# One batch's sums over U and the next batch's first local scores in one group on TensorE, the sums laid out by halves of the channels

## The chip, the cores and the metric

The kernel runs on one core of a Trainium2 chip. The metric is the device time of one execution in microseconds; lower is better. Profiles name the engines: PE (TensorE's matmuls) and PEld (its weight loads), DVE (VectorE), ACT (ScalarE), POOL (GpSimd) and SP, whose queue issues the DMAs.

## What is computed

Sparse attention, a low-rank mix along the sequence, and an MLP, in float32, for 8 batches of 576 positions, 8 heads of 64 channels (512 channels in all):

```python
# attention: heads 0-3 local (the last 32 positions), heads 4-7 strided (positions 32 apart)
scores = q @ k.T / sqrt(64)                      # masked: local or strided
x = softmax(scores) @ v                          # then heads side by side: [8, 576, 512]
# mix along the sequence, rank 32: U [576, 32], V [32, 576]
h = x.transpose(0, 2, 1) @ U @ V
u = x + h.transpose(0, 2, 1)
# MLP over the channels, 512 -> 2048 -> 512
out = u + relu(u @ w_ch1) @ w_ch2
```

## The kernel before

**Blocks.** The 8 x 576 positions are cut into nine blocks of 512: block n has the first 512 positions of batch n, and block 8 the 64 last positions (the tails) of all batches. A block's MLP is 16 steps (fc) of twelve matmuls of the first layer (`ph<-uh,w` and `ph<-ul,w`; u and the weights are split into a high and a low part) and, two steps behind (`LAG`), twelve of the second (`acc<-gh,w`, `acc<-gl,w`), each 128x512. Four evictions `o<-acc,ul` by VectorE end a block's second layer, so they fall into the beginning of the next block.

**Attention beside it.** While block n = 1 to 6 runs, batch b = n + 1 is prepared. A block is 64 ticks (four per fc), and `plan` (at L851) says from which tick a task runs; in a tick `tick` lets each task take a step. TensorE's order is the order of this code (`tensor.on` is true); the other engines and SP are ordered by the scheduler. All small products write the tile px, of which there is one (`ps_x`, two banks of 512 columns; `psx2`).

- "pairs": the four local heads, two at a time. `attention_pair` (L320) loads keys and queries (kT, qT) and values (vt); `masked` (L214) issues 36 score matmuls, each 64 rows by 32 columns of the array, in eight places side by side (two row groups by four column groups) into columns 0 to 319 of both banks; `masked_shifted` (L223) adds the mask, takes the maximum and subtracts it (s_sb); then come the exponential, a transpose (blocks), a store to DRAM (pd), a fetch in another layout (PT), 36 products with the values (`outputs`, px<-vt,PT) and the division into x_loc. Pair 0's scores stand at tick 3, pair 1's at 13, the products at 20 and 34.
- "str" or heads: `strided_heads` (L356), the four strided heads on POOL (products tmp) and VectorE (their sums s_st), from the tick `EARLY` of the block before; results in x_str.
- "mix": `mix_both` (L470), at tick 47 (51 in block 1), forms the sums over U: x (positions x channels) is the moving operand, U the stationary one with 32 columns. The 576 positions are five pieces: four of 128 rows, which go to four column groups, and one of 64, whose four matmuls cover 64 channels each. x_loc and x_str give 256 channels each. The four partial sums (32 partitions each) are added by one copy of ACT and three additions of VectorE (`st<-px`), and split into tst.
- "u0", "u1": `u_local` and `u_strided` multiply by V (`px<-Vst,tst`, two matmuls 96x512 each) and add x (`xT<-px,xT`, `xS<-px,xS`), which gives the next block's u.
- `tail_products` (L604): four Vst matmuls of 64 columns for the 64 last positions of the batch before, in columns 320 to 447 of px, behind the scores of pair 0 (`due`, `tail_out`).

**Buffers.** The pool "att" has seven buffers (`ATT_BUFS`) for kT, qT, s_sb, blocks, PT, xT, xS, tmp, tl and o, each taken as one comes free; vt has one buffer. A product of POOL, an eviction or a load waits until a buffer is free.

Of the kernel before, what the change touches and what calls it, by code (L numbers as in the profile page):

```python
# [7 lines left out]
F32 = mybir.dt.float32  # L8
# [6 lines left out]
ALU = mybir.AluOpType  # L15
AX = mybir.AxisListType
NEG = -1.0e9
B, H, S, D = 8, 8, 576, 64
DM, FF, R = 512, 2048, 32
NCH = S // 32  # L20
# [5 lines left out]
NSP = 2  # L26
LAG = 2
EARLY = 58


ATT_BUFS = 7
# [16 lines left out]
def fused_kernel(ctx, tc, fqk, lqk, lv, eqk, ev, sqkv, U, V, wts, masks, eye, out):  # L48
# [4 lines left out]
    ap_ = ctx.enter_context(tc.tile_pool(name="ap", bufs=1))  # L53
# [24 lines left out]
    def att(shape, name, dtype=F32):  # L78
        return ap_.tile(shape, dtype, name=name, tag="att", bufs=ATT_BUFS)
# [3 lines left out]
    def psx2():  # L83
        banks["n"] += 1
        if banks["prefix"] and banks["n"] % 3:
            return ps_acc.tile([128, 2, 512], F32, name="acc")
        return ps_x.tile([128, 2, 512], F32, name="px")
# [3 lines left out]
    def dma(out, in_):  # L91
        with tc.issue_after(last_dma[0]) if InOrder.on and last_dma[0] is not None else nullcontext():
            last_dma[0] = nc.sync.dma_start(out=out, in_=in_).ins  # L93
# [4 lines left out]
    masks_sb = const.tile([128, 768 + D + 1], BF16, name="masks_sb")  # L98
# [113 lines left out]
    due = []  # L212

    def masked(kT, qT, sp):  # L214
        for c in range(NCH):
            t, c4 = c // 4, c % 4
            for hh, rows in enumerate(halves):
                key = kT[rows, 32 * c - 32:32 * c + 32] if c else kT[rows, None, 0:32].broadcast_to([64, 2, 32])
                tensor.matmul(sp[32 * c4:32 * c4 + 32, hh, 64 * t:64 * t + 64], qT[rows, 32 * c:32 * c + 32], key,
                                 start=True, stop=True, skip_group_check=True, tile_position=(64 * hh, 32 * c4))  # L220
        return sp[:, :, 0:320].rearrange("p h (t x) -> p h t x", x=64)

    def masked_shifted(sp, mask):  # L223
        s_sb = att([128, 5, 2, 64], "s_sb")
        mx = ap_.tile([128, 16], F32, name="mx", bufs=2)[:, 0:10].rearrange("p (h t) -> p h t", h=2)
        s_v = s_sb.rearrange("p t h x -> p h t x")
        m = mask.rearrange("p (t x) -> p t x", x=64)[:, None]
        nc.gpsimd.memset(s_sb[64:128, 4], 0.0)
        for n, ts in ((128, slice(0, 4)), (64, slice(4, 5))):
            vector.tensor_tensor(out=s_v[0:n, :, ts], in0=sp[0:n, :, ts],  # L230
                                 in1=m[0:n, :, ts].broadcast_to([n, 2, ts.stop - ts.start, 64]), op=ALU.add)
        vector.tensor_reduce(out=mx, in_=s_v, axis=AX.X, op=ALU.max)
        vector.tensor_tensor(out=s_v, in0=s_v, in1=mx.broadcast_to([128, 2, 5, 64]), op=ALU.subtract)
        return s_sb

    def shifted(sp):
        s_sb = att([128, 5, 2, 64], "s_sb")
# [6 lines left out]
    def exponentials(s_sb):  # L244
        scalar.activation(out=s_sb, in_=s_sb, func=AF.Exp, scale=0.125)
# [9 lines left out]
    def turned(view, store):  # L255
        blocks = att([128, 640], "blocks")
        vector.transpose(out=blocks.rearrange("p (e t s) -> p t e s", e=4, s=32), in_=view)
        for e in range(4):
            dma(out=store[e].rearrange("k c x -> c k x"), in_=blocks[:, 160 * e:160 * e + 160])

    def fetched(store, name):
        got = att([128, 640], name)
        dma(out=got, in_=store.rearrange("e k c x -> (e k) (c x)"))
        return got
# [36 lines left out]
                vector.tensor_tensor(out=dst, in0=o[:, hh, :, 0:D].rearrange("p t (e x) -> p t e x", e=2),  # L301
                                        in1=rb[:, hh].rearrange("p t (e x) -> p t e x", e=2), op=ALU.mult)

    def pair_loads(b, pr, bufs=None):
        src, values = (lqk[b, pr], lv[b, pr]) if pr < 2 else (eqk[b, pr - 2], ev[b, pr - 2])
        if bufs is None:
            kT, qT = att([128, S], "kT"), att([128, S], "qT")
            full = ap_.tile([128, NCH, D + 1], F32, name="vt", tag="vt")
            dma(out=kT, in_=src[0])
            dma(out=qT, in_=src[1])  # L310
            dma(out=full.rearrange("p c x -> p (c x)"), in_=values)
            return kT, qT, lambda c: full[:, c]
        kT, qT, v0, v1 = bufs
        dma(out=kT, in_=src[0])
        dma(out=qT, in_=src[1])
        for n, part in enumerate((v0, v1)):
            dma(out=part.rearrange("p c x -> p (c x)"), in_=values[:, 9 * (D + 1) * n:9 * (D + 1) * (n + 1)])
        return kT, qT, lambda c: (v0, v1)[c // 9][:, c % 9]

    def attention_pair(b, pr, loaded=None):  # L320
        if loaded is None:
            loaded = pair_loads(b, pr)
            for _ in range(3 + 6 * pr):
                yield
        kT, qT, vt = loaded
        px = psx2()
        sp = masked(kT, qT, px)
        last = due.pop() if due else None
        if last is not None:
            tail_products(last, px)  # L330
        yield
        s_sb = masked_shifted(sp, masks_sb[:, 0:320])
        if last is not None:
            tail_out(last, px)
        yield
        exponentials(s_sb)
        yield
        yield
        turned(s_sb.rearrange("p t h (e x) -> p t (h e) x", x=32), p_store[pr])
        yield  # L340
        yield
        PT = fetched(p_store[pr], "PT")
        for _ in range(11 + 4 * pr):
            yield
        op = outputs(PT, vt, lambda c: 160 * (c % 4) + 32 * (c // 4))
        yield
        normalised(op, pr)
        yield
        turned(x_loc[:, :, 128 * pr:128 * pr + 128].rearrange("p t (e x) -> p t e x", x=32), x_store[pr])
        yield  # L350


# [115 lines left out]
        vector.tensor_tensor(out=dst[64:96], in0=ps, in1=dst[0:32].bitcast(F32), op=ALU.subtract)  # L468

    def mix_both(b):  # L470
        ps = psx2()[:, :, 0:256]
        for half, x in enumerate((x_loc, x_str)):
            for j in range(4):
                tensor.matmul(ps[32 * j:32 * j + 32, half], U_sb[:, 0, j, :], x[:, j, :], start=True, stop=False,
                                 skip_group_check=True, tile_position=(0, 32 * j))
        for half, x in enumerate((x_loc, x_str)):
            for j in range(4):
                part = slice(64 * j, 64 * j + 64)
                tensor.matmul(ps[32 * j:32 * j + 32, half, part], U_sb[0:64, 0, 4, :], x[0:64, 4, part], start=False,
                                 stop=True, skip_group_check=True, tile_position=(0, 32 * j))  # L480
        ta = sums_in[b].rearrange("p (h d) -> p h d", h=2)
        scalar.copy(out=ta, in_=ps[0:32])
        for j in range(1, 4):
            vector.tensor_tensor(out=ta, in0=ps[32 * j:32 * j + 32], in1=ta, op=ALU.add)
        tsts[b] = ap_.tile([96, DM], F32R, name="tst")
        dst = tsts[b].rearrange("p (h d) -> p h d", h=2)
        scalar.copy(out=dst[0:32], in_=ta)
        scalar.copy(out=dst[32:64], in_=ta)
        vector.tensor_tensor(out=dst[64:96], in0=ta, in1=dst[0:32].bitcast(F32), op=ALU.subtract)
# [114 lines left out]
    def tail_products(b, px):  # L604
        for half, ps in enumerate(tail_space(px)):
            for dc in range(2):
                mixed(ps[:, dc], b, 2 * half + dc, Vst, TB, S, True)

    def tail_out(b, px):
        (p0, p1), tl = tail_space(px), tail_of(b)  # L610
        vector.tensor_tensor(out=tl[:, 0:2], in0=p0, in1=tl[:, 0:2], op=ALU.add)
        for e in range(2):
            vector.tensor_tensor(out=tl[:, 2 + e], in0=p1[:, e], in1=o_str[b][e][:, TB:S], op=ALU.add)
        dma(out=rest[:, :, 64 * b:64 * b + 64], in_=tl)
# [209 lines left out]
    def task(gen, key, start, rate=1.0, after=()):  # L824
        return [gen, key, start, rate, after, 0.0]

    def calls(*fns):
        for fn in fns:
            fn()
            yield  # L830

    def plan(n):
        b = n + 1
        if b < B:
            return [
                task(run_staggered([attention_pair(b, 0), attention_pair(b, 1)], 4), "pairs", 0, 1.0),
                task(calls(lambda: mix_both(b)), "mix", 51 if n == 1 else 47, 1.0, ("pairs", "str")),
                task(u_local(b), "u0", 51 if n == 1 else 48, 1.0, ("mix",)),
                task(calls(lambda: u_strided(b), lambda: None, lambda: tail_begin(b)), "u1", 58 if n == 1 else 55, 1.0,
                     ("mix", "u0")),  # L840
            ]
        if b == B:
            return [task(last_tail(), "tail", 2), task(u_rest(), "rest", 12, 1.0, ("tail",))]
        return []
# [216 lines left out]
```

## Time and profile before

| | us |
|---|---|
| median of three runs | 893.72 (893.64 to 895.8) |
| the profiled execution, own time | 894.76 |
| its span on the profile | 892.7 |
| ahead of and behind the span | 2.06 |
| one block (from 333.6 to 428.2 on the profile) | 94.6 |
| scores, all 864 records of `px<-kT,qT` 64x64 | 11.8 busy |
| sums over U, 112 records of 128x256 and 112 of 64x64 | 13.1 busy |

The profile was taken in one execution; the granted clock of TensorE was 0.998. A row of a timeline has the start in us from the span's start, the busy time, the engine, the line (L70 is a helper through which most instructions are issued, so rows are told apart by the tiles), what is written and read, and how many instructions were put together (xN). Float32 matmuls of the attention take two passes, so each is two records. In brackets stands how long the engine idled ahead and what ended it. Busy times of pipelined matmuls overlap; starts are sounder than ends.

### The profile page before, as it was taken

What the parts mean: (1) busy time and instruction counts of PE and PEld (TensorE: products, weight loads), DVE (VectorE), ACT (ScalarE), POOL (GpSimd) and SP (SyncE); (2) the same over time, 40 slices, a digit from 0 to 9 for tenths busy, and PEclk for the clock granted to TensorE, in tenths of its full rate; (3) what the DMA queues carried; (4) which work ended last, traced back from release to release, by engine and by line L of the source; (5) the groups of instructions that cost most, each with busy time, mean ns of one, the idle gap of its engine ahead of it and who ended that gap; (6) DMA issues with size and microseconds to landing.
All of it is one profiled execution on the core that took longest, in us unless ns stands there. A gap on an engine that the chain in (4) does not pass through costs nothing.

```text
span 892.7 us, 16196 instructions
## 1 busy us (share of the span) xinstructions
PE 881.7 (99%) x6625; PEld 708.1 (79%) x6625; DVE 523.9 (59%) x953; ACT 257.8 (29%) x501; POOL 376.9 (42%) x398
## 2 busy tenths in 40 slices
PE   7999999999999999999999999999999999999998
PEld 4677778887878788878888788878887888888886
DVE  5998875766677656766577566756767331112112
ACT  6866751115212521142114311331015221111110
POOL 2000014964796368665668366926854120002000
PEclk9999999999999999999999999999999999999999
DMA  9991111222223223331232313232231030001001
GB/s 353 406 404 63 55 60 54 85 92 71 85 81 121 80 67 97 99 96 59 89 93 77 104 50 121 67 101 60 81 96 48 1 101 0 1 1 48 1 0 48
DMA packets 45914, 80.63 MB, mean 90 GB/s; under 512 B 10736, under 2 KB 23536, under 8 KB 45840
## 3 DMA queue, kind: packets, MB, share of 16 engines
q1 hardware_dynamic: 45840, 79.60, 26.7%
q8 instruction: 52, 0.85, 0.4%
q14 instruction: 22, 0.18, 0.1%
HBM read 61.23 MB, written 18.35 MB: 89 GB/s over the span
## 4 chain that ended last, share of the span: by engine, by line
PE 94%; DVE 2%; DMA 2%; POOL 1%; SPq 1%; issue 0%; DVEq 0%
PE acc L70 44%; PE ph L70 44%; PE px L70 6%; DMA raw_u<-in_U_dram 1%; DMA raw<-in_wts_dram 1%; POOL tmp L374 1%; SPq L93 1%; DVE s_st L70 0%; DVE ul L70 0%; DVE s_sb L70 0%; DVE o L70 0%; DVE xS L70 0%; DVE x_str L70 0%; DVE x_loc L70 0%; DVE mx L70 0%
## 5 line engine op out<-in xcount | busy, mean ns | idle before, releaser
L70 PE MATMUL ph<-uh,w 128*128 128x512 f32 x1152 | 384.8, 392 | 0.0
L70 PE MATMUL acc<-gh,w 128*128 128x512 f32 x1152 | 382.8, 392 | 0.5 <-DVE o L70 0.5
L374 POOL TENSOR_TENSOR tmp<-st,st 128x576 f32<-128x576 f32 (+6 forms) x162 | 175.4, 1112 | 236.9 <-DMA st<-in_sqkv_dram 154.1
L70 PEld LDWEIGHTS acc<-gh,w 128*128 128x128 f32 x1152 | 216.3, 188 | 47.4 <-issue 0.9
L70 PEld LDWEIGHTS ph<-uh,w 128*128 128x128 f32 x1152 | 216.2, 188 | 47.1 <-DVE gl L70 0.5
L70 PE MATMUL ph<-ul,w 128*128 128x512 f32 x576 | 224.3, 389 | 0.0
L70 PE MATMUL acc<-gl,w 128*128 128x512 f32 x576 | 224.3, 389 | 0.0
L70 ACT ACTIVATE gh<-ph 128x512 fp32r<-128x512 f32 x144 | 86.0, 598 | 456.2 <-PE ph L70 450.5
L70 DVE SCALAR_TENSOR_TENSOR gl<-ph,gh 128x512 fp32r<-128x512 f32 x144 | 98.6, 686 | 177.8 <-ACT gh L70 177.4
L400 POOL TENSOR_TENSOR tmp<-st,s_st 128x448 f32<-128x448 f32 (+7 forms) x162 | 137.1, 943 | 52.8 <-DVE s_st L70 30.3
L70 DVE TENSOR_REDUCE s_st<-tmp 128x9 f32<-128x576 f32 (+6 forms) x162 | 90.5, 570 | 59.9 <-POOL tmp L374 56.9
L70 PEld LDWEIGHTS ph<-ul,w 128*128 128x128 f32 x576 | 108.2, 188 | 21.9
L70 PEld LDWEIGHTS acc<-gl,w 128*128 128x128 f32 x576 | 108.1, 188 | 21.8
L70 DVE TENSOR_REDUCE st<-tmp 128x64 f32<-128x64 f32 (+8 forms) x162 | 90.8, 569 | 40.2 <-POOL tmp L400 37.9
L704 POOL TENSOR_TENSOR o<-o,uh 128x512 f32<-128x512 f32 x32 | 40.4, 1297 | 115.1 <-DVE o L70 115.1
L70 ACT COPY x_str<-st 32x256 f32<-32x256 f32 (+1 forms) x144 | 50.5, 351 | 43.1 <-DVE st L70 41.4
L70 ACT ACTIVATE s_sb<-s_sb 128x640 f32<-128x640 f32 x20 | 14.8, 738 | 41.8 <-DVE s_sb L70 39.5
L70 DVE TENSOR_TENSOR st<-px,st 32x512 f32<-32x512 f32 x18 | 12.4, 686 | 21.5 <-ACT st L70 21.1
L70 DVE SCALAR_TENSOR_TENSOR raw<-raw 128x512 int32<-128x512 int32 x32 | 22.0, 688 | 3.7 <-ACT raw L70 3.5
L70 DVE SCALAR_TENSOR_TENSOR cv<-cv,raw 128x512 int32<-128x512 int32 x32 | 22.2, 693 | 1.1
L70 DVE TENSOR_TENSOR w<-cv,w 128x512 fp32r<-128x512 f32 x32 | 21.8, 684 | 0.9 <-ACT w L70 0.9
L70 DVE TENSOR_TENSOR o<-acc,ul 128x512 f32<-128x512 f32 x32 | 20.6, 680 | 2.6 <-DMA out_dram<-o 2.1
(127 smaller groups left out, 484.3 us busy)
## 6 DMA issues: line engine op xcount, KB each, us to landing
raw<-in_wts_dram SPq DMA_DIRECT2D x32, 512.0 KB
st<-in_sqkv_dram SPq DMA_DIRECT2D x18, 576.0 KB
out_dram<-o SPq DMA_DIRECT2D x35, 256.0 KB
vt<-in_lv_dram SPq DMA_DIRECT2D x14, 585.0 KB
pd<-blocks SPq DMA_DIRECT2D x48, 80.0 KB
PT<-pd SPq DMA_DIRECT2D x12, 320.0 KB
xd<-blocks SPq DMA_DIRECT2D x48, 80.0 KB
xT<-xd SPq DMA_DIRECT2D x12, 320.0 KB
```

Source lines behind the costliest of these rows:

```text
L70: r = op(*args, **kwargs)
L93: last_dma[0] = nc.sync.dma_start(out=out, in_=in_).ins
L374: nc.gpsimd.tensor_tensor(out=tmp[:, 0:n], in0=sk[:, j0:j0 + n], in1=sq[:, i:i + 1].broadcast_to([128, n, D]), op=ALU.mult)
L400: nc.gpsimd.tensor_tensor(out=tv.rearrange("p d j -> p j d"), in0=sv[:, 0:i + 1, d0:d0 + step], in1=s_st[:, i, 0:i + 1].broadcast_to([128, ...
L704: nc.gpsimd.tensor_tensor(out=o, in0=o, in1=uh[:, m].bitcast(F32), op=ALU.add)
```

## The change

1. `mix_both(b)` for b = 2 to 6 (blocks 1 to 5) first issues the 36 score matmuls of pair 0 of batch b + 1, into columns 0 to 319 of the same px tile; the sums stand in columns 320 to 447. The keys are loaded by a new task, "keys", at tick 39. `with_mask` (two additions of VectorE) reads the scores right after the sums were added; s_sb is kept until the next block.
2. The sums are laid out by halves of the channels: a column group holds 128 channels of x_loc and of x_str (two banks) for two of the four pieces of positions. Sixteen matmuls of 128 channels replace eight of 256. The last piece has eight matmuls 64 wide as before, now with 128 rows. Two partial sums per half are added: twice a copy of ACT and an addition of VectorE over 256 columns.
3. Timing of the pairs is in a table, `PAIR_TICKS`. For batches whose first scores were early (3 to 7, blocks 2 to 6) pair 0 has no score group of its own; pair 1's scores stand at tick 7 (before 13) and carry the tail's four matmuls; PT is fetched later (own ticks 14 and 28); products stand at 20 and, in the block's ticks, 35.

```diff
+PAIR_TICKS = (((3, 3, 14, 20), (13, 10, 28, 34)), ((2, 2, 14, 20), (6, 5, 28, 34)))
...
+    early_keys, early_scores, early_first = {}, {}, set()
...
+    def attention_pair(b, pr):
+        early, own = b in early_first, {}
...
+        def scores():
+            px = psx2()
+            sp = px[:, :, 0:320].rearrange("p h (t x) -> p h t x", x=64)
+            masked(*own["keys"], sp)
+            last = due.pop() if due else None
+            if last is not None:
+                tail_products(last, px)
+            own["s"] = with_mask(sp, masks_sb[:, 0:320])
...
+        at = PAIR_TICKS[early][pr]
+        if early and pr == 0:
+            steps = [(6, values), (at[0], saved)]
+        else:
+            steps = [(at[0] - at[1], keys), (0 if pr == 0 else 22, values), (at[0], scores)]
+        steps += [(at[0] + 1, lambda: shift(own["s"])), (at[0] + 2, lambda: exponentials(own["s"])), (at[0] + 4, store),
+                  (at[2], fetch), (at[3], products), (at[3] + 1, lambda: normalised(own["o"], pr)), (at[3] + 2, turn_x)]
...
     def mix_both(b):
-        ps = psx2()[:, :, 0:256]
-        for half, x in enumerate((x_loc, x_str)):
-            for j in range(4):
-                tensor.matmul(ps[32 * j:32 * j + 32, half], U_sb[:, 0, j, :], x[:, j, :], start=True, stop=False,
-                                 skip_group_check=True, tile_position=(0, 32 * j))
-        for half, x in enumerate((x_loc, x_str)):
-            for j in range(4):
-                part = slice(64 * j, 64 * j + 64)
-                tensor.matmul(ps[32 * j:32 * j + 32, half, part], U_sb[0:64, 0, 4, :], x[0:64, 4, part], start=False,
-                                 stop=True, skip_group_check=True, tile_position=(0, 32 * j))
-        ta = sums_in[b].rearrange("p (h d) -> p h d", h=2)
-        scalar.copy(out=ta, in_=ps[0:32])
-        for j in range(1, 4):
-            vector.tensor_tensor(out=ta, in0=ps[32 * j:32 * j + 32], in1=ta, op=ALU.add)
+        px = psx2()
+        ps, xs = px[:, :, 320:448], (x_loc, x_str)
+        sp = px[:, :, 0:320].rearrange("p h (t x) -> p h t x", x=64)
+        if b + 1 < B:
+            masked(*early_keys.pop(b + 1), sp)
+        for j in range(4):
+            for half in range(2):
+                for c in range(2):
+                    g = 64 * c + 32 * (j % 2)
+                    tensor.matmul(ps[g:g + 32, half], U_sb[:, 0, j, :], xs[half][:, j, 128 * c:128 * c + 128], start=j < 2,
+                                     stop=False, skip_group_check=True, tile_position=(0, g))
+        for j in range(2):
+            for half in range(2):
+                for c in range(2):
+                    g, x0 = 64 * c + 32 * j, 64 * j
+                    tensor.matmul(ps[g:g + 32, half, x0:x0 + 64], U_sb[:, 0, 4, :],
+                                     xs[half][:, 4, 128 * c + x0:128 * c + x0 + 64], start=False, stop=True,
+                                     skip_group_check=True, tile_position=(0, g))
+        ta = sums_in[b]
+        for c in range(2):
+            half_ta = ta.rearrange("p (h c x) -> p h c x", h=2, c=2)[:, :, c]
+            scalar.copy(out=half_ta, in_=ps[64 * c:64 * c + 32])
+            vector.tensor_tensor(out=half_ta, in0=ps[64 * c + 32:64 * c + 64], in1=half_ta, op=ALU.add)
...
+        if b + 1 < B:
+            early_first.add(b + 1)
+            early_scores[b + 1] = with_mask(sp, masks_sb[:, 0:320])
...
-                task(run_staggered([attention_pair(b, 0), attention_pair(b, 1)], 4), "pairs", 0, 1.0),
-                task(calls(lambda: mix_both(b)), "mix", 51 if n == 1 else 47, 1.0, ("pairs", "str")),
+                task(run_staggered([attention_pair(b, 0), attention_pair(b, 1)], 1), "pairs", 0, 1.0),
+                task(calls(lambda: mix_both(b)), "mix", 51 if n == 1 else 47, 1.0, ("pairs", "str", "keys")),
+                task(calls(lambda: early_keys.update({b + 1: load_keys(b + 1, 0)} if b + 1 < B else {})), "keys", 39, 1.0,
+                     ("pairs",)),
```

The order on PE in the last quarter of block 1 (`w_3`: the MLP's steps 12 to 15; then the part of the weights, and a buffer's number). Before:

```order
L70 MATMUL ph<-uh,w_3_1_1524 128x512
L70 MATMUL ph<-ul,w_3_1_1524 128x512
L70 MATMUL ph<-uh,w_3_1_1524 128x512
L70 MATMUL px<-x_loc,U_sb 32x256 x4
L70 MATMUL px<-x_str,U_sb 32x256 x4
L70 MATMUL px<-x_loc,U_sb 32x64 x4
L70 MATMUL px<-x_str,U_sb 32x64 x4
L70 MATMUL ph<-uh,w_3_2_1405 128x512
```

With the change, whose helper lines are one further down (the sums' rows alternate on between x_loc and x_str, four times 128 wide and twice 64 wide):

```order
L71 MATMUL ph<-ul,w_3_1_1524 128x512
L71 MATMUL ph<-uh,w_3_1_1524 128x512
L71 MATMUL px<-kT,qT 32x64 x36
L71 MATMUL px<-x_loc,U_sb 32x128 x2
L71 MATMUL px<-x_str,U_sb 32x128 x2
...
L71 MATMUL px<-x_loc,U_sb 32x64 x2
L71 MATMUL px<-x_str,U_sb 32x64 x2
L71 MATMUL ph<-uh,w_3_2_1405 128x512
```

The scores stand ahead of the sums in one group between the same two steps of the MLP. On PE at the beginning of block 2, where the second layer of block 1 ends and the first of block 2's begins its round (`w_0_0`), before:

```order
L70 MATMUL acc<-gl,w_3_2_1711 128x512
L70 MATMUL acc<-gh,w_3_2_1711 128x512
L70 MATMUL px<-kT,qT 32x64 x36
L70 MATMUL px<-Vst,tst 128x64 x4
L70 MATMUL ph<-uh,w_0_0_479 128x512
L70 MATMUL ph<-ul,w_0_0_479 128x512
```

With the change:

```order
L71 MATMUL acc<-gl,w_3_3_1731 128x512
L71 MATMUL acc<-gh,w_3_3_1731 128x512
L71 MATMUL px<-kT,qT 32x64 x36
L71 MATMUL px<-Vst,tst 128x64 x4
L71 MATMUL ph<-uh,w_0_0_479 128x512
L71 MATMUL ph<-ul,w_0_0_479 128x512
```

There the first group was pair 0's; it is now pair 1's, one step of the MLP later (`w_3_3` for `w_3_2`), and pair 0 has none. On DVE at the evictions of the same block start (acc_1986 and acc_1987, acc_1982 and acc_1983 are the two accumulators of the second layer, s_sb_2867 and s_sb_2680 are pair 0's scores, s_sb_2982 pair 1's), before:

```order
L70 TENSOR_TENSOR s_sb_2867<-s_sb_2867,mx_2868 128x2x5x64
L70 TENSOR_REDUCE s_st_2706<-tmp_2887 128x9
L70 SCALAR_TENSOR_TENSOR gl_2897<-ph_2860,gh_2896 128x512
L70 TENSOR_REDUCE s_st_2706<-tmp_2901 128x3
L70 TENSOR_TENSOR o_2922<-acc_1986,ul_1362 128x512
L70 TENSOR_REDUCE s_st_2706<-tmp_2910 128x9
L70 TENSOR_TENSOR o_2926<-acc_1986,ul_1362 128x512
L70 TENSOR_REDUCE s_st_2706<-tmp_2913 128x4
L70 TENSOR_TENSOR o_2930<-acc_1987,ul_1362 128x512
L70 TENSOR_TENSOR o_2934<-acc_1987,ul_1362 128x512
L70 SCALAR_TENSOR_TENSOR gl_2964<-ph_2947,gh_2963 128x512
L70 STREAM_TRANSPOSE blocks_2938<-s_sb_2867 128x5x4x32
```

With the change:

```order
L71 TENSOR_REDUCE s_st_2758<-tmp_2896 128x3
L71 STREAM_TRANSPOSE blocks_2907<-s_sb_2680 128x5x4x32
L71 TENSOR_TENSOR o_2925<-acc_1982,ul_1362 128x512
L71 TENSOR_REDUCE s_st_2758<-tmp_2913 128x9
L71 TENSOR_REDUCE s_st_2758<-tmp_2916 128x4
L71 TENSOR_TENSOR o_2929<-acc_1982,ul_1362 128x512
L71 TENSOR_TENSOR o_2933<-acc_1983,ul_1362 128x512
L71 SCALAR_TENSOR_TENSOR gl_3013<-ph_2993,gh_3012 128x512
L71 TENSOR_TENSOR o_2937<-acc_1983,ul_1362 128x512
L71 TENSOR_TENSOR s_sb_2982<-px_2941,masks_sb_83 128x2x4x64
L71 TENSOR_TENSOR s_sb_2982<-px_2941,masks_sb_83 64x128
L71 TENSOR_TENSOR tl_2803<-px_2941,tl_2803 128x128
```

Pair 0's transpose now stands ahead of the evictions and pair 1's mask behind them; the second eviction stands behind two reductions of POOL's products instead of one each. The mask, maximum and subtraction of pair 0 moved back into block 1, behind the sums.

More of the change, by code (lines that the diff above doesn't have):

```diff
@@ L218, in masked, with with_mask @@
                 key = kT[rows, 32 * c - 32:32 * c + 32] if c else kT[rows, None, 0:32].broadcast_to([64, 2, 32])
-                tensor.matmul(sp[32 * c4:32 * c4 + 32, hh, 64 * t:64 * t + 64], qT[rows, 32 * c:32 * c + 32], key,
+                tensor.matmul(sp[32 * c4:32 * c4 + 32, hh, t], qT[rows, 32 * c:32 * c + 32], key,
                                  start=True, stop=True, skip_group_check=True, tile_position=(64 * hh, 32 * c4))
-        return sp[:, :, 0:320].rearrange("p h (t x) -> p h t x", x=64)
-    def masked_shifted(sp, mask):
+    def with_mask(sp, mask):
         s_sb = att([128, 5, 2, 64], "s_sb")
-        mx = ap_.tile([128, 16], F32, name="mx", bufs=2)[:, 0:10].rearrange("p (h t) -> p h t", h=2)
         s_v = s_sb.rearrange("p t h x -> p h t x")
@@ L231, in masked_shifted, with shift @@
                                  in1=m[0:n, :, ts].broadcast_to([n, 2, ts.stop - ts.start, 64]), op=ALU.add)
+        return s_sb
+    def shift(s_sb):
+        mx = ap_.tile([128, 16], F32, name="mx", bufs=2)[:, 0:10].rearrange("p (h t) -> p h t", h=2)
+        s_v = s_sb.rearrange("p t h x -> p h t x")
         vector.tensor_reduce(out=mx, in_=s_v, axis=AX.X, op=ALU.max)
         vector.tensor_tensor(out=s_v, in0=s_v, in1=mx.broadcast_to([128, 2, 5, 64]), op=ALU.subtract)
-        return s_sb
     def shifted(sp):
@@ L302, in normalised @@
                                         in1=rb[:, hh].rearrange("p t (e x) -> p t e x", e=2), op=ALU.mult)
[L304 to L323, printed above, removed]
-                yield
[L325 to L349, printed above, removed]
+    early_keys, early_scores, early_first = {}, {}, set()
@@ new lines, in load_keys, with load_values, keys, values @@
+    def load_keys(b, pr):
+        kT, qT = att([128, S], "kT"), att([128, S], "qT")
+        for x in range(2):
+            dma(out=(kT, qT)[x], in_=lqk[b, pr, x])
+        return kT, qT
+    def load_values(b, pr):
+        full = ap_.tile([128, NCH, D + 1], F32, name="vt", tag="vt")
+        dma(out=full.rearrange("p c x -> p (c x)"), in_=lv[b, pr])
+        return lambda c: full[:, c]
+    def attention_pair(b, pr):
+        early, own = b in early_first, {}
+        def keys():
+            own["keys"] = load_keys(b, pr)
+        def values():
+            own["vt"] = load_values(b, pr)
+        def scores():
[6 more added lines that the diff above has]
+            own["s"] = with_mask(sp, masks_sb[:, 0:320])
+            if last is not None:
+                tail_out(last, px)
+        def saved():
+            own["s"] = early_scores.pop(b)
+        def store():
+            turned(own["s"].rearrange("p t h (e x) -> p t (h e) x", x=32), p_store[pr])
+        def fetch():
+            own["PT"] = fetched(p_store[pr], "PT")
+        def products():
+            own["o"] = outputs(own["PT"], own["vt"], lambda c: 160 * (c % 4) + 32 * (c // 4))
+        def turn_x():
+            turned(x_loc[:, :, 128 * pr:128 * pr + 128].rearrange("p t (e x) -> p t e x", x=32), x_store[pr])
+        at = PAIR_TICKS[early][pr]
[5 more added lines that the diff above has]
+                  (at[2], fetch), (at[3], products), (at[3] + 1, lambda: normalised(own["o"], pr)), (at[3] + 2, turn_x)]
+        now = 0
+        for when, step in sorted(steps, key=lambda z: z[0]):
+            while now < when:
+                now += 1
+                yield
+            step()
@@ L485, in mix_both @@
+        ta = ta.rearrange("p (h d) -> p h d", h=2)
+        if b + 1 < B:
+            early_first.add(b + 1)
+            early_scores[b + 1] = with_mask(sp, masks_sb[:, 0:320])
         tsts[b] = ap_.tile([96, DM], F32R, name="tst")
```

## Prediction

> **What bounds the kernel now.** I read the page first: the busy time of each engine, then the chain of work that ended last.
>
> ```profile
> PE 881.7 (99%) x6625; PEld 708.1 (79%) x6625; DVE 523.9 (59%) x953; ACT 257.8 (29%) x501; POOL 376.9 (42%) x398
> ...
> PE 94%; DVE 2%; DMA 2%; POOL 1%; SPq 1%; issue 0%; DVEq 0%
> PE acc L70 44%; PE ph L70 44%; PE px L70 6%; DMA raw_u<-in_U_dram 1%; DMA raw<-in_wts_dram 1%; POOL tmp L374 1%; SPq L93 1%; DVE s_st L70 0%; DVE ul L70 0%; DVE s_sb L70 0%; DVE o L70 0%; DVE xS L70 0%; DVE x_str L70 0%; DVE x_loc L70 0%; DVE mx L70 0%
> ```
>
> TensorE is the bound: 94% of the chain is PE, and only 6% of it are the px groups that the change touches; DVE, busy 59%, matters where PE waits for it. So I price the edit by what each px group costs between two matmuls of the MLP. The timeline of PE shows that, first for pair 1's scores of block 3 (the start in us, the modelled time of the row, what it is):
>
> ```profile
> 349.77 0.39 PE L70 MATMUL ph<-ul,w 128*128 128x512 f32 x1
> 350.00 0.39 PE L70 MATMUL ph<-uh,w 128*128 128x512 f32 x1
> 350.31 0.97 PE L70 MATMUL px<-kT,qT 64*32 64x64 f32 x72
> 351.21 0.50 PE L70 MATMUL acc<-gh,w 128*128 128x512 f32 x1
> 351.55 0.39 PE L70 MATMUL acc<-gl,w 128*128 128x512 f32 x1
> ```
>
> The starts count, since the ends are modelled. An MLP matmul follows another after 350.00 - 349.77 = 0.23 us. The scores begin 0.31 after the last one (0.08 more than the pitch), hold PE for 351.21 - 350.31 = 0.90, and the second MLP matmul behind them comes 0.34 after the first (0.11 more). So a score group costs 0.90 and an **entry and exit of 0.19**, 1.09 us in all. The sums over U of the same batch, in the same view:
>
> ```profile
> 305.01 0.39 PE L70 MATMUL acc<-gh,w 128*128 128x512 f32 x1
> 305.33 0.64 PE L70 MATMUL px<-x_loc,U_sb 128*32 128x256 f32 x8
> 305.78 0.62 PE L70 MATMUL px<-x_str,U_sb 128*32 128x256 f32 x8
> 306.33 0.32 PE L70 MATMUL px<-x_loc,U_sb 64*32 64x64 f32 x8
> 306.47 0.29 PE L70 MATMUL px<-x_str,U_sb 64*32 64x64 f32 x8
> 306.69 0.50 PE L70 MATMUL ph<-uh,w 128*128 128x512 f32 x1
> ```
>
> They hold PE for 306.69 - 305.33 = 1.36; with the same 0.19 of entry and exit (the entry is 305.33 - 305.01 here) that is 1.55. Inside, the four matmuls of x_loc (two passes each, so x8) take 0.45. The same four of x_str take 0.55 before the 64-row matmuls begin: **0.10 goes to the change from 128 to 64 rows**. The last four take 0.22, the four before them 0.14: 0.08 goes to the change back to the MLP's form.
>
> **The change, part by part.**
>
> *One group instead of two (blocks 1 to 5).* Pair 0's 36 score matmuls no longer stand alone, but ahead of the sums. The 0.90 of the scores, which holds the change to the next form, stays, and one entry and exit of 0.19 goes: 5 x 0.19 = 0.95 us. The lower bound is 0, if the entry of the sums costs the same behind scores as behind an MLP matmul. The upper bound comes from the scores' own end. When the Vst matmuls follow the scores, they also start 0.90 after them, as this pair of rows of block 2 shows:
>
> ```profile
> 239.43 0.97 PE L70 MATMUL px<-kT,qT 64*32 64x64 f32 x72
> 240.33 0.63 PE L70 MATMUL px<-Vst,tst 96*128 96x64 f32 x4
> ```
>
> so a form change inside a group does cost something like the 0.10 above; were it free, 5 x 0.29 = 1.45 would go. I take 0.95: this pair of rows is of the same operation, followed by another group.
>
> The tail's four Vst matmuls move from pair 0's group to pair 1's; these are the same four matmuls in a group that is entered anyway: nothing.
>
> *The sums by halves of the channels (blocks 1 to 6).* Sixteen matmuls of 128 channels replace eight of 256; each of the four column groups still streams 2 x 256 channels. Side by side that is again 2 x 0.45 = 0.90. The eight last ones are 64 wide as before, but all have 128 rows, so that the 0.10 of the form change goes: 6 x 0.10 = 0.60. Below, the eight extra weight loads could show: 32 records in 0.90 us are one per 28 ns. The last matmuls of before ran eight records in 0.14 us, one per 18 ns, though with 64 rows, which speaks for room. I keep 0 for the extra loads, with 6 x 0.15 = 0.9 lost as the far end (were the eight weight loads of 18 ns each to stand in the open), and 6 x 0.18 = 1.1 gained as the other (both form changes gone).
>
> Whether four column groups stream side by side in the new order of the code is seen best against a stretch of the first batch in which one column group works alone, ten passes of 128 columns (the last two with 64 rows):
>
> ```profile
> 32.49 1.39 PE L70 MATMUL ph<-x_loc,U_sb 128*32 128x128 f32 x10
> 33.81 0.44 PE L70 MATMUL px<-ident,x_loc 128*128 128x128 f32 x2
> ```
>
> Alone a pass takes 1.32/10 = 0.13 for 128 columns; the old sums needed 0.45/8 = 0.06 for 256. So four groups run beside each other there, though each matmul's second pass must wait for its first. The Trainium skill, "TensorE: Matmul & The Clock Gate", Part 3 (What overlaps and what doesn't), says that matmuls start and end strictly in program order, without reordering. By that rule the order of groups 0, 64, 0, 64 and then 32, 96, 32, 96 would leave at most two of four streaming, and the whole would be the +5.5 of the third rival; by the rows it is the -1.55 worked out below.
>
> *Partial sums.* ACT and DVE now do two copies and two additions of 256 columns for one copy and three additions of 512, and then DVE adds the mask to the scores, ahead of what the path needs:
>
> ```profile
> 306.87 0.58 ACT L70 COPY st<-px 32x512 f32<-32x512 f32 x1 [3.49 <-PE px L70]
> 307.48 2.13 DVE L70 TENSOR_TENSOR st<-px,st 32x512 f32<-32x512 f32 x3 [3.38 <-ACT st L70]
> 311.17 0.68 DVE L70 TENSOR_TENSOR tst<-st,tst 32x512 fp32r<-32x512 f32 x1
> 314.31 1.29 DVE L70 TENSOR_TENSOR xT<-px,xT 128x512 f32<-128x512 f32 x2 [2.46 <-PE px L70]
> 313.64 0.64 PE L70 MATMUL px<-Vst,tst 96*128 96x512 f32 x2
> 318.22 0.64 PE L70 MATMUL px<-Vst,tst 96*128 96x512 f32 x2
> L70 DVE TENSOR_TENSOR s_sb<-px,masks_sb 128x512 f32<-128x512 f32 x12 | 8.3, 690 | 13.9 <-PE px L70 13.5
> L70 DVE TENSOR_TENSOR s_sb<-px,masks_sb 64x128 f32<-64x128 f32 x12 | 3.3, 272 | 0.0
> L70 DVE TENSOR_REDUCE mx<-s_sb 128x10 f32<-128x640 f32 x12 | 9.7, 805 | 0.0
> L70 DVE TENSOR_TENSOR s_sb<-s_sb,mx 128x640 f32<-128x640 f32 x12 | 12.5, 1038 | 0.2
> ```
>
> The scores ahead delay the sums by 0.90. The three additions took 2.13, two half-wide ones should take some 0.71 (a third of it), and the mask adds 0.69 + 0.27 = 0.96: 0.90 + 0.71 + 0.96 - 2.13 = 0.44 later at most. tst was whole at 311.17 + 0.68 = 311.85, and the Vst matmuls that read it started at 313.64: 1.79 of cover, so nothing. The maximum and subtraction (0.81 + 1.04) stand before the two xT additions, which ended at 315.60; px is wanted again at 318.22. In the 2.46 that DVE idled before 314.31 they fit. Ahead of the xT additions now also stands the first reduction of the strided heads, which waits for a load. If these rows lose all cover, u_strided's Vst matmuls wait, some 0.5 us a block; I take 0.
>
> *The block starts.* Four operations of DVE that stood ahead of the evictions o<-acc move away from there; pair 1's stand behind them. The timelines of POOL, DVE and PE at the start of block 2:
>
> ```profile
> 245.48 3.27 POOL L374 TENSOR_TENSOR tmp<-st,st 128x192 f32<-128x192 f32 x3
> 249.49 0.40 DVE L70 TENSOR_REDUCE s_st<-tmp 128x4 f32<-128x256 f32 x1
> 249.82 1.27 DVE L70 TENSOR_TENSOR o<-acc,ul 128x512 f32<-128x512 f32 x2
> 248.86 0.39 PE L70 MATMUL ph<-uh,w 128*128 128x512 f32 x1
> 249.72 0.47 PE L70 MATMUL acc<-gh,w 128*128 128x512 f32 x1 [0.47 <-DVE o L70]
> ```
>
> 249.72 - 248.86 less the pitch of 0.23 is **0.63 that PE lost** to the second eviction. The mask, maximum and subtraction (0.96 + 0.81 + 1.04 = 2.81) leave this stretch. But the pool of seven buffers is tighter: pair 0's s_sb now crosses the block's start, and the next products of POOL wait for a buffer of pair 1's keys. Its scores stand at tick 7 where pair 0's (239.43, above) stood at tick 3; a tick is 94.6/64 = 1.48, so they start near 245.3 and, 0.90 later and a little more, free it near 246.3. Two products of 1.09 (3.27/3), a reduction of 0.40, and an eviction of 0.68 give 249.6, and PE could start near 249.7: the very moment of before. I take the stall as unchanged, 0; its ends are -0.6 (gone) and +1.1 (one product more ahead of it). In blocks 3 to 6 the heads run earlier against the block's start, and PE lost nothing there, by the windows of the two blocks (window, its us, busy us of PE, PEld, DVE, ACT and POOL with instructions, PE's clock, DMA share, GB/s):
>
> ```profile
> 239.00:333.60 94.60, 94.13 (x709) 75.90 (x708) 65.30 (x124) 24.02 (x50) 63.04 (x67) 1.00 0.28 89
> 333.60:428.20 94.60, 94.60 (x714) 76.81 (x713) 63.42 (x120) 24.03 (x50) 60.48 (x63) 1.00 0.28 86
> ```
>
> PE is busy 94.60 of 94.60 us in block 3 and 94.13 in block 2, which is the 0.47 of idle time in the row above.
>
> *DMAs.* The same loads, stores and fetches are issued, but pair 0's fetch of PT now stands behind pair 1's four stores on SP:
>
> ```profile
> 254.14 1.66 SPq L93 DMA_DIRECT2D pd<-blocks  x3
> 259.39 0.33 SPq L93 DMA_DIRECT2D PT<-pd  x1
> 266.34 0.97 PE L70 MATMUL px<-vt,PT 64*32 64x65 f32 x72
> ```
>
> The fetch of before was issued 6.95 ahead of the products. Four stores are 4 x 0.55 = 2.2 of SP's time; were pair 1's s_sb itself late, 2.81 of DVE's work more lies ahead. Some 2 us are left, so nothing; without that cover each us late is a us lost.
>
> The sum: -0.95 - 0.60 + 0 = **-1.55 us** on the profiled execution (its own time 894.76, so 893.2). That execution lies 1.04 above the median of the runs shown, 893.72, from which I forecast: 893.72 - 1.55 = **892.2**. By the bounds of the groups and the stall: -(1.45 + 1.1 + 0.6) = -3.2, and 0 - 0.6 + 0.9 + 1.1 = +1.4, so 890.5 to 895.1.
>
> **The rivals.**
> - *More goes: the stall too, and the form changes in the groups.* For it: 2.81 us of DVE's work leave the stretch before the stall. Against it: POOL's buffers. -3.2, 890.5. Chance 0.14.
> - *Merging brings nothing*: the sums' entry costs as much behind scores as behind the MLP, and the extra weight loads eat the row change. For it: scores end with the same 0.90 before any follower. About 0: 893.7. Chance 0.22.
> - *Slower: the new sums run only two column groups side by side.* The new order is groups 0, 64, 0, 64, then 32, 96, 32, 96; the old one was 0, 32, 64, 96. If a matmul that waits for its column group holds back those behind it, only two of four stream: the main part takes 1.80 instead of 0.90, the last part 0.28 more, six times 1.18 less the 1.55: +5.5, 899.2. It decides as soon as fewer than nine passes can be looked ahead of a waiting one. Against it: the 0.06 against 0.13 above, in an order that needed a look ahead too. Chance 0.07.
> - *Slower: stalls at every block's start.* Evictions wait for the buffers that s_sb and pair 1's keys hold, in blocks 2 to 6, one POOL product (1.09) each: 5 x 1.09 - 1.55 = +3.9, 897.6. It decides as soon as the second eviction ends after the MLP's second layer should start. For it: the 0.63 in block 2. Against it: block 3's full PE row. Chance 0.08.
>
> **How the numbers follow.** The forecast has 0.49, with a range of its own from 891.2 to 893.3. The range of 890.4 to 895.3 leaves out the two slower cases (0.15) and the far end of the faster one (0.05). What a measurement of this kernel tells from no change is 0.3%, 2.7 us: faster is below 891.0, the first rival and the edge of the forecast, 0.17; slower is above 896.4, the two slower cases where they are whole, 0.12; the same 0.71.
>
> **What would show it.** In PE's timeline of the changed kernel the merged group should run 0.90 from the scores to the sums and 1.26 from the sums to the MLP, against 1.36; if the sums take above 2, the column groups don't overlap. The gap near 249.4 should stand at about 0.6, with no other in blocks 3 to 6. A DVE wait before xT<-px or a PE wait at u_strided's Vst matmuls would show that the cover there is gone. I am wrong if the px groups shrink as forecast and the span doesn't, or if a new PE wait of over 1 us appears.

## The result and the profile after

| | before | changed |
|---|---|---|
| median, us | 894.55 (6 runs, 893.3 to 896.39) | 907.81 (6 runs, 905.71 to 909.22) |
| ratio, 95% interval | | 1.0135 (1.0118 to 1.0151): slower |
| span of the profiled execution, us | 892.7 | 907.4 |

The change made the kernel 13 us slower, and the forecast of 892.2 (890.4 to 895.3) missed. The profile of the changed kernel, its busy line and its chain:

```profile
PE 884.8 (98%) x6721; PEld 715.6 (79%) x6721; DVE 514.8 (57%) x947; ACT 258.2 (28%) x507; POOL 377.3 (42%) x398
...
PE 82%; POOL 6%; DMA 4%; DVE 3%; issue 2%; SPq 1%; ACT 1%; DVEq 0%; POOLq 0%; ACTq 0%
PE acc L71 38%; PE ph L71 38%; PE px L71 6%; POOL tmp L392 5%; DMA pd<-blocks 1%; SPq L94 1%; DVE s_st L71 1%; DMA PT<-pd 1%; DMA scr<-in_fqk_dram 1%; POOL o L735 1%; DVE blocks L71 0%; DMA st<-in_sqkv_dram 0%; DVE o L71 0%; POOL ul L582 0%; DVE xT L71 0%
```

PE's share of the chain fell from 94 to 82%, and POOL, DVE and the DMAs pd and PT took it: PE now waits for work that lay beside it before. Its share by px stayed at 6%, so the groups themselves did not grow. The merged group of block 2 in PE's timeline:

```profile
310.00 0.39 PE L71 MATMUL acc<-gh,w 128*128 128x512 f32 x1
310.31 0.97 PE L71 MATMUL px<-kT,qT 64*32 64x64 f32 x72
311.21 0.44 PE L71 MATMUL px<-x_loc,U_sb 128*32 128x128 f32 x8
311.45 0.41 PE L71 MATMUL px<-x_str,U_sb 128*32 128x128 f32 x8
311.67 0.42 PE L71 MATMUL px<-x_loc,U_sb 128*32 128x128 f32 x8
311.89 0.42 PE L71 MATMUL px<-x_str,U_sb 128*32 128x128 f32 x8
312.11 0.32 PE L71 MATMUL px<-x_loc,U_sb 128*32 128x64 f32 x8
312.22 0.32 PE L71 MATMUL px<-x_str,U_sb 128*32 128x64 f32 x8
312.47 0.50 PE L71 MATMUL ph<-uh,w 128*128 128x512 f32 x1
```

Scores to sums 0.90, sums to the MLP 312.47 - 311.21 = 1.26: both as forecast. The time went elsewhere, which the windows of blocks show. They are cut at the 769th, 1153rd, 1537th, 1921st, 2305th and 2689th MLP matmul (window, its us, busy us of PE, PEld, DVE, ACT and POOL with instructions, PE's clock, DMA share, GB/s):

```profile
241.02:340.80 99.78, 96.46 (x729) 78.38 (x728) 64.04 (x123) 24.05 (x51) 64.10 (x67) 0.98 0.27 84
340.80:438.93 98.13, 95.91 (x730) 78.56 (x728) 61.96 (x119) 24.07 (x51) 60.64 (x64) 0.98 0.26 83
438.93:535.01 96.08, 94.35 (x730) 77.42 (x728) 61.85 (x118) 23.95 (x51) 60.58 (x64) 1.00 0.27 85
535.01:633.28 98.27, 95.97 (x730) 78.58 (x729) 61.60 (x118) 24.06 (x51) 60.22 (x64) 0.98 0.27 83
633.28:729.16 95.88, 93.90 (x662) 77.06 (x661) 53.23 (x103) 23.33 (x50) 46.26 (x47) 1.00 0.17 54
```

All five blocks lost, the first one most: 488.14 us together. The same windows of the kernel before are 95.70, 94.62, 94.62, 94.66 and 94.00, together 473.60: 14.5 us of the 14.7 between the spans. PE's timeline names the waits, first at the start of block 2, then in block 3 (which the later blocks repeat; the last row is block 6's):

```profile
250.54 0.39 PE L71 MATMUL ph<-uh,w 128*128 128x512 f32 x1
251.61 0.47 PE L71 MATMUL acc<-gh,w 128*128 128x512 f32 x1 [0.69 <-ACT gh L71]
...
252.84 0.40 PE L71 MATMUL acc<-gh,w 128*128 128x512 f32 x1
255.87 0.50 PE L71 MATMUL acc<-gh,w 128*128 128x512 f32 x1 [2.64 <-DVE o L71]
...
365.28 0.39 PE L71 MATMUL ph<-uh,w 128*128 128x512 f32 x1
367.89 0.96 PE L71 MATMUL px<-vt,PT 64*32 64x65 f32 x72 [2.22 <-issue]
...
660.12 0.96 PE L71 MATMUL px<-vt,PT 64*32 64x65 f32 x72 [1.98 <-DMA PT<-pd]
```

In block 2 PE lost 251.61 - 250.54 - 0.23 = 0.84 and 255.87 - 252.84 - 0.23 = 2.80 waiting for evictions (before: 0.63). For the first of these two the row names ACT's gh; I read it as the second eviction all the same, since that ended at 251.46, 0.15 ahead of PE, as in the kernel before (249.57 for 249.72). In block 3 it lost 367.89 - 365.28 - 0.32 = 2.29 ahead of pair 0's products. The profile says "issue" there, but in block 6 it names the fetch of PT for the same wait. So the fetch has to be followed in the queues. SP and DVE in block 3:

```profile
348.80 2.48 DVE L71 TENSOR_TENSOR o<-acc,ul 128x512 f32<-128x512 f32 x4 [2.36 <-DMA pd<-blocks]
353.04 0.88 DVE L71 TENSOR_TENSOR s_sb<-px,masks_sb 128x512 f32<-128x512 f32 x2 [1.75 <-DMA out_dram<-o]
...
360.79 2.26 SPq L94 DMA_DIRECT2D pd<-blocks  x4
363.21 0.38 SPq L94 DMA_DIRECT2D PT<-pd  x1
```

Pair 0's fetch of PT is issued at 363.21, right behind pair 1's four stores, and the products start 4.7 us later (367.89 - 363.21). The stores are late, because pair 1's s_sb is written only at 353.04, although its scores began at 346.3: DVE first waited 2.36 us with the evictions for the stores of pair 0 (which free one of the seven buffers), and then 1.75 us with the mask for the stores of the evicted o (which free another).

So two theories stood against each other. **A, the order on SP:** the fetch must not stand behind pair 1's stores. **B, the buffers:** pair 0's s_sb, carried over the start of the block, leaves too few of the seven, and everything behind the evictions is late. Each might be the cause alone.

### The profile page after: what moved, and what is told of

The parts are those of the page before. It is cut to its first block, busy times and chain, and to the rows that moved or that the text cites. A ratio compares the mean times of both kernels' runs of the same rounds, so it can differ in the third digit from the quotient of the medians.

```text
span 907.4 us, 16377 instructions
## 1 busy us (share of the span) xinstructions
PE 884.8 (98%) x6721; PEld 715.6 (79%) x6721; DVE 514.8 (57%) x947; ACT 258.2 (28%) x507; POOL 377.3 (42%) x398
## 4 chain that ended last, share of the span: by engine, by line
PE 82%; POOL 6%; DMA 4%; DVE 3%; issue 2%; SPq 1%; ACT 1%; DVEq 0%; POOLq 0%; ACTq 0%
PE acc L71 38%; PE ph L71 38%; PE px L71 6%; POOL tmp L392 5%; DMA pd<-blocks 1%; SPq L94 1%; DVE s_st L71 1%; DMA PT<-pd 1%; DMA scr<-in_fqk_dram 1%; POOL o L735 1%; DVE blocks L71 0%; DMA st<-in_sqkv_dram 0%; DVE o L71 0%; POOL ul L582 0%; DVE xT L71 0%
## 5 line engine op out<-in xcount | busy, mean ns | idle before, releaser
L71 DVE TENSOR_REDUCE st<-tmp 128x64 f32<-128x64 f32 (+8 forms) x162 | 88.9, 568 | 20.1 <-POOL tmp L418 19.0
L71 ACT ACTIVATE s_sb<-s_sb 128x640 f32<-128x640 f32 x20 | 14.7, 737 | 51.6 <-DVE s_sb L71 43.2
L71 DVE TENSOR_TENSOR o<-acc,ul 128x512 f32<-128x512 f32 x32 | 20.4, 685 | 14.5 <-DMA pd<-blocks 11.8
L582 POOL TENSOR_TENSOR ul<-xT,uh 128x512 fp32r<-128x512 f32 x12 | 15.5, 1298 | 25.7 <-ACT uh L71 25.7
L71 PEld LDWEIGHTS px<-vt,PT 64*32 64x32 f32 x1152 | 13.1, 105 | 14.0 <-issue 13.0
L71 PE MATMUL px<-vt,PT 64*32 64x65 f32 x1152 | 15.6, 225 | 8.2 <-issue 4.5
```

Source lines behind the costliest of these rows:

```text
L71: r = op(*args, **kwargs)
L582: nc.gpsimd.tensor_tensor(out=ul, in0=src, in1=uh.bitcast(F32), op=ALU.subtract)
```

## The experiments

**The fetch earlier.** Only the fetch is moved, ahead of pair 1's stores:

```diff
-((2, 2, 14, 20), (6, 5, 28, 34))
+((2, 2, 9, 20), (6, 5, 28, 34))
```

> Only pair 0's fetch of PT is moved from its own tick 14 to 9, ahead of pair 1's four stores on SP. Theory A (the fetch stands behind stores that are late): the PE waits ahead of px<-vt,PT in blocks 3 to 6 (2.1 to 2.7 us each, and the half rate after them) go, 907.8 falls by 10 to 12 to about 896, and block 2 keeps its waits of 0.85 and 2.81 for the evictions. Theory B (seven buffers are too few at the block's start): PT now takes a buffer early, the evictions or pair 1's s_sb wait for one instead, PE's waits move to acc<-gh, and the time stays within 3 us of 907.8.

896.18 against 895.01 of before (ratio 1.0013, 1.0004 to 1.0022). Blocks 3 to 6 had no PE wait left; block 2 had its two, and the half rate after them. As theory A said. SP in block 3, whose pair 1 scores began at 344.1 in this run:

```profile
353.55 0.33 SPq L94 DMA_DIRECT2D PT<-pd  x1
358.53 2.24 SPq L94 DMA_DIRECT2D pd<-blocks  x4
```

The fetch leads now. Pair 1's stores still come as late after its scores, 14.4 us (changed kernel: 360.79 - 346.3 = 14.5), but nothing of pair 0 is behind them. So the late buffers alone cost nothing in these blocks.

**Pair 0's stores earlier.** The fetch stays where the change put it:

```diff
-((2, 2, 14, 20), (6, 5, 28, 34))
+((-4, -4, 14, 20), (6, 5, 28, 34))
```

> Pair 0's transpose and stores six ticks earlier (own tick 0 instead of 6), the fetch left at 14 behind pair 1's stores. Theory A: block 2's 2.81 goes, since the fourth eviction waited for these stores, but the PE waits ahead of px<-vt,PT in blocks 3 to 6 stay above 1.5 us: about 904. Theory B: the evictions no longer wait for the stores (2.4 us on DVE in block 3), pair 1's chain and its stores come as much earlier, and the waits ahead of px<-vt,PT fall below 0.5 us: 893 to 897.

893.89 against 895.01 (ratio 0.9991, 0.9978 to 1.0003). Blocks 3 to 6 were free of waits here too, as theory B said. DVE and SP in block 3 (pair 1's scores began at 343.7):

```profile
342.43 1.29 DVE L71 TENSOR_TENSOR o<-acc,ul 128x512 f32<-128x512 f32 x2
344.69 1.29 DVE L71 TENSOR_TENSOR o<-acc,ul 128x512 f32<-128x512 f32 x2 [0.97 <-PE px L71]
346.71 0.88 DVE L71 TENSOR_TENSOR s_sb<-px,masks_sb 128x512 f32<-128x512 f32 x2 [0.73 <-DMA out_dram<-o]
...
352.79 2.24 SPq L94 DMA_DIRECT2D pd<-blocks  x4
355.20 0.38 SPq L94 DMA_DIRECT2D PT<-pd  x1
```

The fetch is still behind pair 1's stores, 11.5 us after its scores. In the changed kernel it was 363.21 - 346.3 = 16.9, and the products waited 2.3; so up to about 14.6 would have been hidden. Neither theory alone is the cause: **the wait needs both**, the stores late by buffers and the fetch queued behind them, and it goes when either goes. In block 2 the fourth eviction's wait went, but PE now waited 2.45 for the second one, and 0.83 came ahead of the products. POOL's timeline of this block shows why: the strided heads' products stood still until pair 0's stores freed a buffer, and the evictions stand behind their reductions:

```profile
243.89 2.12 POOL L392 TENSOR_TENSOR tmp<-st,st 128x64 f32<-128x64 f32 x3 [3.53 <-DMA pd<-blocks]
```

**Pair 1 back at tick 13.** The scores where they were, the keys still loaded at tick 4:

```diff
-((2, 2, 14, 20), (6, 5, 28, 34))
+((2, 2, 9, 20), (12, 9, 28, 34))
```

> Pair 0's fetch at tick 9 and pair 1's scores back at tick 13 (keys four ticks ahead), as before the change; the merged group stays. Theory A: as with the fetch alone, about 896, block 2's waits stay, since pair 0's stores stand where they stood. Theory B: neither pair 1's keys nor its s_sb ask for a buffer among the evictions, so block 2's 2.81 falls below 1 as well: 892 to 894.

925.89 (ratio 1.0348, 1.0328 to 1.0369): both theories as I had put them missed, by 30 us. PE waited for evictions in every block. The expectation speaks of keys four ticks ahead; this edit loads them nine ahead, as the kernel before did. Two rows of DVE in block 3:

```profile
354.64 1.29 DVE L71 TENSOR_TENSOR o<-acc,ul 128x512 f32<-128x512 f32 x2 [1.75 <-DMA pd<-blocks]
359.51 0.69 DVE L71 TENSOR_TENSOR o<-acc,ul 128x512 f32<-128x512 f32 x1 [3.58 <-DMA out_dram<-o]
```

I had overlooked that the keys and queries, loaded at tick 4, sit in two of the seven buffers until tick 13. They did so before the change as well, where PE waited only 0.63 us, in block 2; what the merged group holds beside them is new (this difference is argued, not tested by itself). To test this, they were loaded three ticks ahead of the scores, not nine:

```diff
-((2, 2, 9, 20), (12, 9, 28, 34))
+((2, 2, 9, 20), (12, 3, 28, 34))
```

> Like the run with pair 1's scores at tick 13 (925.9), but its keys are loaded three ticks ahead of them instead of nine. If the keys that lie in two buffers over the evictions made those 31 us, the waits at acc<-gh in blocks 3 to 6 (1.1 to 4.2) fall below 0.5 and the time is 893 to 899. If pair 0's PT or the late tail (its buffers held until tick 13) did, they stay above 1.5 us and the time above 910.

923.69 in a single run. The waits at the evictions were gone in all blocks, as said; but the loads of the keys then came late (kT issued at 353.78 in block 3), and PE waited 4 us ahead of pair 1's scores in each of the five blocks:

```profile
353.78 0.34 SPq L94 DMA_DIRECT2D kT<-in_lqk_dram  x1
355.44 0.33 SPq L94 DMA_DIRECT2D qT<-in_lqk_dram  x1
```

So the waits at the evictions needed the two buffers of the keys, and my number for the time was wrong: the same lack came out in another place. The keys waited for buffers, not for SP's time: the fetch ahead of them was issued at 351.85 and took 0.33, SP then stood idle, and by the profile it waited 1.5 us ahead of kT and 1.2 ahead of qT for DVE's reductions, which free the buffers of POOL's products.

**The layout alone.** No scores are merged, the pairs keep the old ticks (the first condition stands in one more place):

```diff
-        if b + 1 < B:
+        if False:
...
-                task(calls(lambda: early_keys.update({b + 1: load_keys(b + 1, 0)} if b + 1 < B else {})), "keys", 39, 1.0,
+                task(calls(lambda: None), "keys", 39, 1.0,
```

> The sums over U in halves of the channels alone; no score group is merged, and the pairs keep the old ticks (pair 1's scores one tick later). Both theories: 1.26 us from the first sum to the MLP against 1.36, six times 0.10 less than the kernel before, no new PE wait over 0.3 us: 893.3 to 894.5 beside 894.5.

892.67 against 895.01 (ratio 0.9971, 0.996 to 0.9982): faster than expected by a little. Its sums took 1.26 in the trace, as in the merged group:

```profile
305.86 0.44 PE L71 MATMUL px<-x_loc,U_sb 128*32 128x128 f32 x8
...
307.12 0.50 PE L71 MATMUL ph<-uh,w 128*128 128x512 f32 x1
```

Between the 590th and the 2689th MLP matmul the two traces differ by 1.79 us (516.39 against 518.18). 0.60 of it are the six sums. Block 2's wait shrank from 0.63 to 0.39, the longer score group there (1.09 instead of 0.90) became normal, and a gap of 0.19 at 678 went; that is 0.62 more. The rest, some 0.6, is spread over small gaps.

**No merged group in block 1.** The remaining wait of block 2 is avoided, and both the stores and the fetch are early (the condition stands in two more places):

```diff
-((2, 2, 14, 20), (6, 5, 28, 34))
+((-4, -4, 9, 20), (6, 5, 28, 34))
...
-        if b + 1 < B:
+        if 2 < b < B - 1:
```

> No merged group in block 1 (batch 3 starts as before the change), in the others pair 0's stores six ticks and its fetch five ticks earlier. If block 2's stall (2.45 and 0.83 in the run with early stores) comes from pair 0's s_sb among the buffers there, where the strided heads start late, it falls to the 0.4 of the layout alone, and four merged groups gain 0.2 to 0.3 each over the layout alone: 891 to 892.5 beside 895. If it comes from the heads' late start alone, block 2 keeps over 2 us: 893 to 895.

892.09 against 894.92 (ratio 0.9966, 0.9955 to 0.9978), block 2's wait 0.42. So the merged group of block 1 made block 2 wait. Without it, though, pair 1's scores of block 2 stand at their old tick too; the next run, which merges all five groups and keeps them at tick 7, tells these apart.

**The early scores stored in the block before.** All five groups are merged, but pair 0's maximum, exponential, transpose and stores follow the sums at once, so that only DRAM carries them over:

```diff
+    def early_store(b):
+        if b in early_scores:
+            s_sb = early_scores.pop(b)
+            shift(s_sb)
+            yield
+            exponentials(s_sb)
+            yield
+            yield
+            turned(s_sb.rearrange("p t h (e x) -> p t (h e) x", x=32), p_store[0])
+        yield
...
+                task(early_store(b + 1), "early", 56 if n == 1 else 52, 1.0, ("mix",)),
```

(with the fetch at tick 9, and pair 0's own steps up to the store removed)

> All five groups merged; pair 0's maximum, exponential, transpose and stores come in the block before (tick 52, 56 in block 1), the fetch at tick 9 ahead of pair 1's stores. Theory B (buffers held over the block's start): only DRAM carries the early scores, block 2's stall falls below 1 us and blocks 3 to 6 have none: 890 to 892.5. Rival: the additional work of DVE and SP in the block's last part, ahead of xT<-px and the loads of st, makes u_strided or the heads late: new waits at px<-Vst,tst, 893 to 897.

891.19 against 894.92 (ratio 0.9959, 0.9947 to 0.9971). The rival's waits didn't come, and no gap over 0.6 us is left in blocks 1 to 6. POOL's wait for pair 0's stores ahead of block 2 is 0.76, where it was 3.53 with the stores at tick 0. So it was the carried s_sb, with the buffers that its late stores hold, that made block 2 wait. Windows of blocks 2 to 4:

```profile
240.65:334.92 94.27, 94.27 (x729) 77.38 (x728) 65.90 (x125) 24.07 (x51) 65.97 (x70) 1.00 0.28 89
334.92:429.20 94.28, 94.28 (x730) 77.39 (x728) 63.42 (x119) 24.29 (x51) 60.21 (x64) 1.00 0.28 86
429.20:523.47 94.27, 94.27 (x729) 77.38 (x728) 62.97 (x119) 24.17 (x51) 60.34 (x64) 1.00 0.28 86
```

PE is busy all the time. This version beats both kernels. Its interval overlaps that of the layout alone, so the times don't rank these two; the traces do, by 94.28 against 94.49 us for block 3.

## Why the prediction was wrong

*The groups: right.* Forecast -0.95 by merging and -0.60 by the layout. Block 3 took 94.62 before, 94.49 with the layout alone and 94.28 with merging too, without a wait in any of them: 0.13 and 0.21, where I had 0.10 and 0.19.

*The slower rival of two column groups: refuted.* The sums would have taken above 2 us and took 1.26. The strict order that the Trainium skill states ("TensorE: Matmul & The Clock Gate", Part 3, What overlaps and what doesn't) doesn't hold here: in the program two matmuls of x_loc (groups 0 and 64) are followed by two of x_str in the same groups and only then by x_loc's in 32 and 96, but in the trace x_loc's eight passes start ahead of x_str's first, and each eight take 0.22 to 0.24, where a lone pass took 0.13.

*The partial sums: right.* No wait arose at px<-Vst,tst.

*The step on the DMAs failed.* It said: "Some 2 us are left, so nothing". I saw that the fetch is queued behind pair 1's stores, took those for 2.2 us of SP's time and up to 2.81 of DVE's, and did not follow when they could start at all. Their data were held up by two buffer waits (2.36 and 1.75), the evictions between them and DVE's reductions of POOL's products, 14.5 us from the scores to the stores. That cost PE 1.8 to 2.4 us in each of blocks 3 to 6, 8.5 together. The chain was no faster before, as SP's row of pair 1's stores in block 3 of that kernel shows; nothing that was needed soon stood behind it:

```profile
365.29 2.49 SPq L93 DMA_DIRECT2D pd<-blocks  x4
```

Its scores began at 350.31, 15.0 us earlier. And the 6.95 us from fetch to products were not all cover, since a fetch needs some 4.7 itself (363.21 to 367.89 above). From these rows an estimate for block 3 comes out near: 346.3 + 15.0 + 2.4 (stores to fetch) + 4.7 = 368.4 for the products, where PE was ready at 365.6, so 2.8 late; it was 2.29.

*The step on the block starts failed as well.* "I take the stall as unchanged, 0; its ends are -0.6 (gone) and +1.1": it grew by 3.0. I had counted POOL's products ahead of the second eviction; the wait that came last was that of the fourth for a buffer that pair 0's stores free, 4.2 us after they were issued. And I gave the rival of buffer waits at each block's start 0.08 with the evictions as its place; buffers were the cause in block 2 and one of two needed causes in blocks 3 to 6, where the place was a fetch.

*A term was missing: the clock.* The sum has no price for it. After three of the six waits PE ran at half rate for some 3.5 us (MLP matmuls 0.43 apart, not 0.23); the rows at 466.40 and 661.00 are the two stretches in which it did not:

```profile
255.87:259.40 3.53, 3.52 (x9) 2.82 (x10) 3.10 (x7) 0.00 (x0) 3.36 (x4) 0.57 0.34 105
368.70:372.20 3.50, 3.50 (x18) 2.65 (x9) 2.89 (x11) 1.03 (x2) 0.00 (x0) 0.54 0.85 294
466.40:470.00 3.60, 3.60 (x20) 2.95 (x17) 2.99 (x11) 1.08 (x2) 0.00 (x0) 1.00 0.89 309
563.00:566.60 3.60, 3.60 (x18) 2.82 (x10) 2.99 (x13) 1.07 (x2) 0.31 (x2) 0.58 0.78 266
661.00:664.50 3.50, 3.50 (x19) 2.91 (x16) 2.89 (x11) 1.07 (x2) 0.00 (x0) 1.00 0.86 283
```

The sum against the version without stalls, over the five blocks: 488.14 - 470.94 = 17.2 us. Of that 3.6 (block 2) and 8.5 (blocks 3 to 6) are waits, 4.7 is what the slowed matmuls took more, and 0.4 is spread. The version without stalls is 2.7 below the kernel before in these blocks, which leaves the 14.5.

## What to carry to other kernels

Where a step only moves a DMA behind others in a queue, the price isn't the issue time of those others but the moment at which the last of them may start: follow each back to its data and to the buffer that its data need. A value kept over a busy stretch costs a buffer for that whole stretch; here writing it out early brought more (891.19) than moving the fetch ahead (896.18). A stall is to be priced with what the clock does after it: here 4.7 us on top of 12.1.

## What the runs showed of the hardware

Waits of PE (start to start) of 3.03, 2.60 and 2.69 us were followed by a granted clock of 0.57, 0.54 and 0.58 over some 3.5 us, which cost 1.4 to 1.7 us each (4.7 in all); waits of 2.12 and 2.37 in the same execution weren't, and neither was one of 2.67 in the run with early stores (clock 1.00 from 252.67 to 256.20). So no length of the wait alone decides in this range. In blocks 2 to 6 of all the runs every wait from 2.86 us up, twelve of them, was followed by a clock of 0.50 to 0.62. The Trainium skill, "TensorE: Matmul & The Clock Gate", Part 1, has a free-running window of 3.4 us, after an idle one of which the clock is halved; the 3.5 us of half rate and the dependence on more than the length agree with such a window, but these three waits were all shorter than it, and by that rule none of them would have been enough; the measurement decides.
